# Computing both halves of V for three chunks ahead, and turning the fourth x chunk by a DMA

## The chip, the cores and the metric

One core of a Trainium2 chip. The metric is the device time of one execution in microseconds (us); the span in a profile is the time from its first to its last instruction, some 1.7 us less. Kernels that ran once are of unknown state: their times are told, but what follows is taken from their traces, with the granted clock of TensorE (the share of its full speed that the chip allowed it) where it matters. In lines of a profile, PE is TensorE and PEld its weight loads, ACT is ScalarE, DVE VectorE, POOL GpSimd, and SPq the queue that issues the DMAs; a timeline line gives the start and the duration in us, and in brackets the idle time before it and what ended it.

## The reference, cut to what matters

```python
h  = x + A(layernorm(x))          # memory-augmented attention, 32 heads of 32, 4 segments of 512 tokens
h2 = h + B(layernorm(h))          # gated MLP with a 2048 x 2048 spatial mix
# inside A, for the 2048 tokens of width 1024:
q = x @ wq ; k = x @ wk ; v = x @ wv
# per segment: causal softmax(q k^T) v, mixed with a memory read, memory updated; then o @ wo
```

All tensors are bf16. Segment 0 consists of four chunks of 128 tokens; each has to be normalized and turned (transposed) before Q, K and V of it can be computed.

## The kernel before

The kernel writes down operations in program order with their reads and writes; TensorE keeps that order, the other engines get a fixed order from a list scheduler. The start stage is a string, one word per piece of TensorE work: `T`/`t` is a half chunk turned by four TensorE transposes (copied out by VectorE or ScalarE), `v20` is the first of eight matmuls of chunk 2 with the first half (512 columns) of wv.

```python
LOAD = '12ab3'          # x1, x2, first wv half in two pieces, x3 (x0 goes ahead of them)
START = 'T00 t01 v00 v01 v02 v03 t10 T11 v04 ... v07 v10 ... v14 T20 T21 v15 ... v24 T30 T31 v25 v26 v27 v30 ... v37'
# ...
w_half(WQ, A_wq, 0)
w_half(WK, A_wk, 0)
w_half(WV, A_wv, 1)     # second wv half, last
```

The attention stage is a loop over 16 pairs (a, b) of head groups. Each pair has five steps, and each step begins with logits into PSUM banks 0 to 3, which ScalarE reads in one exponential. Groups of eight matmuls that are not urgent (`v_group`, `wo_group`) fill the steps:

```python
def logits(parts):                      # L464: row-tiled matmuls into banks 0..3
    ...
    act(o, src, ACTF.Exp, scale=float(SCALE))     # one exponential of 128 x 2048

FILL = [  # groups, and the slot (after which step) of each
    (vf((0, 0, 1)) + vf((0, 1, 1)) + vf((0, 2, 1)) + vf((0, 3, 1), eng=DVE), (0, 1, 2, 4,)),   # pair 0
    (vf((1, 0, 0)) + vf((1, 0, 1), eng=DVE), (2, 4,)),                                          # pair 1
    # ...
]
for pair in range(16):
    logits([(a, 0, 0)]);              Pq(b); filler(0);  X(a - 1)             # step 1
    logits([(a, 1, 128), (a, 3, 0)]); Pk(b); MZU(a - 1); phi(b); filler(1)    # step 2
    chores(a)                         # with n < 4: x_norm(4 + n); x_turn(4 + n)
    logits([(a, 2, 0), (b, 2, 256)]); Pq(b + 1); filler(2)                    # step 3
    logits([(b, 0, 0)]);              Pk(b + 1); phi(b + 1); X(a); filler(3)  # step 4
    logits([(b, 1, 128), (b, 3, 0)]); MZU(a); filler(4)                       # step 5
```

(Conditions for the first and last pair are cut. X and MZU are the products with V and the memory update, many matmuls of 33 or 132 columns.)

The softmax here doesn't subtract the row's maximum and nothing guards it: scores larger than these inputs give would overflow.

## Time and profile before

| | before |
|---|---|
| median of the first 3 runs | 796.34 us (796.32 to 800.05) |
| span of the profile | 794.5 us |
| TensorE busy | 99%, granted clock 1.000 |
| TensorE waits in the trace | 2.3 us, all before 9.52 us |
| first logits | 20.03 us |

A table of busy shares says little here, since TensorE is busy all the time.

### The profile page before, as it was taken

Reading aid. Unit: us, or ns where it says so; the run is one execution under the profiler, and the core shown is the slowest. Engines: PE = TensorE matmul, PEld = TensorE weight load, DVE = VectorE, ACT = ScalarE, POOL = GpSimd, SP = SyncE. Lnnn points to the kernel's source line nnn. Section 1 sums busy time; section 2 is a strip of 40 time slices with the busy share of each in tenths; the row PEclk is TensorE's granted clock in tenths of the full one; section 3 lists DMA queues with packets and bytes.
Section 4 is the critical chain, followed back from the end, with each engine's and each line's share of the span. In section 5 each row is a group of like instructions: output and inputs, shape, how many; then the busy total and the mean of one; then the engine's idle time right before and its main releaser. Section 6 shows DMA issues by size and latency. Waiting matters only on the chain.

```text
span 794.5 us, 12077 instructions
## 1 busy us (share of the span) xinstructions
PE 789.9 (99%) x5377; PEld 322.2 (41%) x4773; DVE 373.1 (47%) x857; ACT 289.8 (36%) x341; POOL 140.1 (18%) x266
## 2 busy tenths in 40 slices
PE   8999999999999999999999999999999999999998
PEld 3455554555554542341322314443244334424433
DVE  5784788768765686804215051132233223322322
ACT  5788977777778862132323323100000000000000
POOL 0454535433443341200001010000000000000000
PEclk9999999999999999999999999999999999999999
DMA  9677524622423658510000116603310530011001
GB/s 302 147 142 172 136 54 87 136 65 69 86 54 87 173 124 211 157 40 1 1 0 1 31 34 156 184 1 82 106 32 1 119 100 1 0 55 60 0 1 54
DMA packets 128471, 64.77 MB, mean 82 GB/s; under 512 B 95520, under 2 KB 120352, under 8 KB 128416
## 3 DMA queue, kind: packets, MB, share of 16 engines
q1 hardware_dynamic: 128416, 63.99, 32.7%
q8 instruction: 40, 0.66, 0.3%
q14 instruction: 15, 0.12, 0.1%
HBM read 32.51 MB, written 8.39 MB: 51 GB/s over the span
## 4 chain that ended last, share of the span: by engine, by line
PE 99%; DMA 1%; SPq 0%; issue 0%; DVE 0%
PE ps L327 81%; PE ps L328 14%; PE ps L464 3%; DMA wv<-in_A_wv_dram 1%; SPq L516 0%; PE ps L468 0%; DVE hx L495 0%
## 5 line engine op out<-in xcount | busy, mean ns | idle before, releaser
L327 PE MATMUL ps<-wspT,z 128*128 128x512 bf16 x896 | 194.0, 379 | 0.0
L473 ACT ACTIVATE e<-ps 128x2048 bf16<-128x2048 f32 x80 | 149.8, 1873 | 40.0 <-PE ps L464 40.0
L327 PEld LDWEIGHTS ps<-wspT,z 128*128 128x128 bf16 x896 | 87.7, 98 | 106.4 <-issue 1.0
L473 ACT ACTIVATE z<-ps 128x512 bf16<-128x512 f32 x120 | 63.1, 571 | 145.4 <-PE ps L327 145.4
L495 DVE TENSOR_TENSOR tg<-ps,brow 128x512 bf16<-128x512 f32 x56 | 38.7, 692 | 149.9 <-PE ps L327 122.6
L698 POOL TENSOR_SCALAR_AFFINE_SELECT e<-e 128x1024 bf16<-128x1024 bf16 (+1 forms) x80 | 77.3, 967 | 133.4 <-ACT e L473 133.1
L327 PE MATMUL ps<-hnT,win 128*128 128x512 bf16 x448 | 97.3, 379 | 0.0
L328 PE MATMUL ps<-win,hnT 128*128 128x512 bf16 (+1 forms) x384 | 90.1, 344 | 0.0
L327 PE MATMUL ps<-wout,y 128*128 128x512 bf16 (+2 forms) x252 | 85.8, 367 | 0.0
L568 DVE BATCH_NORM_STATS2 stats<-z 128x6 f32<-128x448 bf16 x64 | 40.1, 627 | 97.0 <-ACT z L473 95.4
L495 DVE TENSOR_TENSOR hx<-hx,ps 128x512 bf16<-128x512 bf16 (+1 forms) x65 | 42.2, 674 | 81.6 <-PE ps L327 81.4
L328 PE MATMUL ps<-wout,y 128*128 128x512 bf16 x210 | 79.6, 379 | 0.0
L327 PEld LDWEIGHTS ps<-hnT,win 128*128 128x128 bf16 x448 | 43.8, 98 | 54.2 <-issue 2.0
L327 PE MATMUL ps<-wv,xnT 128*128 128x512 bf16 x256 | 60.3, 379 | 1.1 <-DMA wv<-in_A_wv_dram 1.1
L327 PE MATMUL ps<-xnT,wk 128*128 128x512 bf16 (+2 forms) x264 | 60.8, 374 | 0.0
L327 PE MATMUL ps<-xnT,wq 128*128 128x512 bf16 x256 | 60.8, 380 | 0.0
L327 PE MATMUL ps<-wo,oT 128*128 128x512 bf16 x256 | 58.8, 379 | 0.0
L327 PEld LDWEIGHTS ps<-wout,y 128*128 128x128 bf16 x252 | 24.2, 98 | 72.2 <-issue 69.1
L327 PE MATMUL ps<-win,hnT 128*128 128x512 bf16 x128 | 48.5, 379 | 0.0
L327 PEld LDWEIGHTS ps<-win,hnT 128*128 128x128 bf16 x128 | 12.5, 98 | 81.4 <-issue 80.9
L327 PEld LDWEIGHTS ps<-v,e 128*128 128x128 bf16 x1280 | 40.1, 96 | 9.8 <-issue 1.7
L327 PE MATMUL ps<-v,e 128*128 128x33 bf16 x1280 | 42.1, 177 | 0.0
(72 smaller groups left out, 609.6 us busy)
## 6 DMA issues: line engine op xcount, KB each, us to landing
win<-in_B_w_in_dram SPq DMA_DIRECT2D x6, 1024.0 KB, 5.3
hx<-in_A_x_dram SPq DMA_DIRECT2D x16, 256.0 KB, 2.8
out_dram<-hx SPq DMA_DIRECT2D x16, 256.0 KB, 2.3
hx<-out_dram SPq DMA_DIRECT2D x16, 256.0 KB, 2.6
out_dram<-hx SPq DMA_DIRECT2D x31, 128.0 KB, 1.7
xin<-in_A_x_dram SPq DMA_DIRECT2D x15, 256.0 KB, 4.0
wout<-in_B_w_out_dram SPq DMA_DIRECT2D x2, 1792.0 KB, 10.1
wq<-in_A_wq_dram SPq DMA_DIRECT2D x2, 1024.0 KB, 7.3
```

What stands on the lines that cost most here:

```text
L327: return e.matmul(out, lhsT, rhs, start=start, stop=stop)
L328: return e.add_instruction(mybir.InstMatmult(name="I-%d" % (1000000 + o.idx), engine=e.engine, ins=[e.lower_ap(rhs), e.lower_ap(lhsT)], ou ...
L464: G.op(PE, lambda e: e.matmul(o, lhsT, rhs, start=True, stop=True, tile_position=(32 * i, 0)), [lhsT, rhs], [o], n / 2.4 if last else 3.5, ...
L473: G.op(ACT, lambda e: e.activation(o, i, func, scale=scale, **kw), r, [o], ((172 if inps(i) else 224) + n_of(i)) / 1.2 + 26, prio=prio, na ...
L495: G.op(DVE, lambda e: e.tensor_tensor(o, a, b, op), [a, b], [o], vcost(o, [a, b], fast), name="tt", prio=late[0])
L568: G.op(DVE, lambda e, si=si, so=so: e.bn_stats(so, si), [si], [so], (cs + 143) / 0.96, name="bn_stats", prio=late[0])
L698: G.op(POOL, lambda e: e.affine_select(d, d, pat, ALU.is_ge, 0.0, base=0, channel_multiplier=-1), [d], [d], 1270 if j else 640, name="mask")
```

## The change

Its intent: let three second-half V groups do in the start what they did among the fillers, and use the time that they take to turn chunk 3 by a DMA instead of on TensorE. For that the second wv half is loaded earlier, the transpose is issued ahead of wk, and chunks 4 to 7 are normalized and turned ahead of pair 0. The filler lists are shifted to fit.

```diff
-    LOAD = '12ab3'
+    LOAD = "12ab3h"                       # h: second wv half
-    START = '... v24 T30 T31 v25 v26 v27 v30 ... v37'
+    START = '... v24 v25 v26 v27 u00 ... u07 u10 ... u17 u20 ... u27 v30 ... v37'
     w_half(WQ, A_wq, 0)
-    w_half(WK, A_wk, 0)
-    w_half(WV, A_wv, 1)
     dma(BETAB[:], A_beta.partition_broadcast(128))
 ...
+    x_turn(3)                             # DMA transpose of chunk 3
+    w_half(WK, A_wk, 0)
+    G.ops[-1].deps.add(first[3] + 5)      # wk waits for chunk 3's norm, so it queues behind the transpose
 ...
     for tc in range(4, 8):
         x_load(tc)
+        G.ops[-1].deps.add(first[3] + 5)
+    for tc in range(4, 8):
+        x_norm(tc)
+        x_turn(tc)
     FILL = [
-        (vf((0, 0, 1)) + vf((0, 1, 1)) + vf((0, 2, 1)) + vf((0, 3, 1), eng=DVE), (0, 1, 2, 4,)),
-        (vf((1, 0, 0)) + vf((1, 0, 1), eng=DVE), (2, 4,)),
+        (vf((0, 3, 1)) + vf((1, 0, 1), eng=DVE) + vf((1, 0, 0)), (0, 1, 4,)),
 ...                                       # 52 groups before, 49 after
```

## The prediction

> **What bounds the kernel now.** I read the page first (busy shares, then the chain that ended last), then what TensorE waited for, then the timeline of the first 45 us, then the DMA issues, their landings and the bytes moved in 2 us stretches.
>
> ```profile
> span 794.5 us, 12077 instructions
> PE 789.9 (99%) x5377; PEld 322.2 (41%) x4773; DVE 373.1 (47%) x857; ACT 289.8 (36%) x341; POOL 140.1 (18%) x266
> ...
> PE 99%; DMA 1%; SPq 0%; issue 0%; DVE 0%
> ```
>
> The chain that ended last is TensorE for 99% of the span. Busy is modelled, so I checked it with TensorE's own waits over the whole run, of which there are only two kinds:
>
> ```profile
> PE ps L327 <- DVE zero L531: 1.2, 1, 1.2
> PE ps L327 <- DMA wv<-in_A_wv_dram: 1.1, 2, 0.7
> ```
>
> Both lie before 9.52 us. From there on the start stage, which the change rewrites, is gapless (view: timeline of TensorE):
>
> ```profile
> 9.52 2.12 PE L327 MATMUL ps<-wv,xnT 128*128 128x512 bf16 x9 [0.35 <-DMA wv<-in_A_wv_dram]
> 11.47 0.61 PE L468 MATMUL ps<-ident,xin 128*128 128x128 bf16 x8
> 11.91 1.89 PE L327 MATMUL ps<-wv,xnT 128*128 128x512 bf16 x8
> 13.64 0.61 PE L468 MATMUL ps<-ident,xin 128*128 128x128 bf16 x8
> 14.09 2.54 PE L327 MATMUL ps<-wv,xnT 128*128 128x512 bf16 x11
> 16.46 1.89 PE L327 MATMUL ps<-xnT,wq 128*128 128x512 bf16 x8
> ```
>
> Read the starts, not the durations, which overlap: 8 matmuls of 512 columns take 13.64 - 11.91 = 1.73 us, 216 ns each; the 8 transposes of chunk 3 take 14.09 - 13.64 = 0.45 us, 56 ns each. The attention stage is as tight. I cut it into steps at the logits (line L464). With 16 wide matmuls a step always takes 3.88 to 3.90 us; with 8 of them and 24 of 33 columns 2.75 or 2.76; a filler group of 8 always adds 1.73. Steps of equal content never differ by more than 0.02 us up to 288 us, so nothing waits there. Here are two kinds of step, and ScalarE in them (timeline, some rows left out):
>
> ```profile
> 27.81 0.40 PE L464 MATMUL ps<-qk 32*128 32x256 bf16 x8
> ...
> 28.14 1.90 PE L327 MATMUL ps<-xnT,wq 128*128 128x512 bf16 x8
> ...
> 29.87 1.89 PE L327 MATMUL ps<-wv,xnT 128*128 128x512 bf16 x8
> ...
> 31.70 0.39 PE L464 MATMUL ps<-qk 32*128 32x512 bf16 x4
> ...
> 37.25 0.39 PE L464 MATMUL ps<-qk 32*128 32x512 bf16 x4
> ...
> 37.70 1.88 ACT L473 ACTIVATE e<-ps 128x2048 bf16<-128x2048 f32 x1 [0.40 <-PE ps L464]
> ```
>
> The step from 27.81 to 31.70 holds one Q group and one filler. The last two lines give the second bound of a step: the exponential starts 0.45 us after its logits and takes 1.88, and the next logits go into the same four PSUM banks.
>
> **What the Trainium skill says.** "TensorE: Matmul & The Clock Gate", section "Wait — 56ns, not 53.3ns?": warm matmuls start every columns / 2.4 GHz plus about 2.5 ns, 55.6 ns at 128 columns and 215.7 at 512. The trace agrees (56 and 216 ns). The same page, "Part 4: PE-mode transpose", gives about 275 ns for a transpose in a kernel. The page of this profile has a mean of 243 ns for them, but in a train only 56 ns pass from one to the next, so 0.45 us is what eight of them cost. "DMA: Bandwidth & Descriptors", section "Queues, rings and completion order": each DMA engine consumes its ring's descriptors in order. The trace agrees: adding up bytes in issue order predicts the landings (below). "Perfetto Trace Analysis", section "DMA Instruction — HWDGE (DVE, Sync)": a DMA's recorded span is the issue only, not the movement; here the wk load is 1.71 us long in the queue's timeline and lands 11.5 us after its issue.
>
> **The change part by part.** (1) Removed from TensorE: T30 and T31, 8 transposes: -0.45 us. Two DVE copies of 0.42 us go too, off the path. (2) Moved: three V groups, u0, u1 and u2 (24 matmuls, 24 x 216 ns = 5.18 us), from the filler lists to the start. I counted the lists: 52 filler groups before, 49 after. So the start grows by 5.18 us, the attention pairs shrink by 5.18 us, net zero as long as every step stays bound by TensorE. (3) Added: one DMA transpose of x chunk 3, off TensorE if it lands in time. (4) The loads are reordered: second wv half, wq, then the transpose, then wk and x chunks 4 to 7.
>
> Does (3) or (4) make TensorE wait? Queue and bytes before:
>
> ```profile
> 2.64 0.98 SPq L516 DMA_DIRECT2D wv<-in_A_wv_dram  x2
> 3.67 0.51 SPq L516 DMA_DIRECT2D xin<-in_A_x_dram  x1
> 4.21 0.43 SPq L516 DMA_DIRECT2D wq<-in_A_wq_dram  x1
> 4.69 1.71 SPq L516 DMA_DIRECT2D wk<-in_A_wk_dram  x1
> 6.44 3.90 SPq L516 DMA_DIRECT2D wv<-in_A_wv_dram  x1
> ```
>
> The 2 us stretches move 15, 241, 324, 299, 349, 376, 349, 348, 348 and 375 GB/s from 0 to 20 us. Summed, 3.15 MB (x0 to x3, first wv half, wq) has gone by 11.8 us and wq landed at 4.21 + 9.0 = 13.2; 4.19 MB by 14.8, and wk landed at 4.69 + 11.5 = 16.2; 5.24 MB by 17.9, and the second wv half landed at 6.44 + 12.7 = 19.1. So a landing is the byte count plus 1.3 us. New order, as estimates from these numbers:
> - second wv half takes wq's place: lands 13.2. u00 is due when v27 ends: 13.64 + 3 x 0.216 = 14.29. Margin 1.1 us.
> - wq takes wk's place: 16.2, due at 21.2. Harmless.
> - the transpose can issue when chunk 3 is normalized, at 12.76 + 0.55 = 13.31 (now followed by the x loads at 13.36). wq's bytes are ahead of it until 14.8, 1.4 us. Transposes of such a chunk land 3.1 at least and 3.4 us in the median after their issue, so it lands at 16.5 to 18.2. v30 is due at 14.29 + 5.18 = 19.47. Margin 1.3 us or more.
> - wk: 1.05 MB at 0.35 MB/us behind the transpose: about 20.3; due at 19.47 + 2 x 1.73 = 22.93. Margin 2.6 us.
> - x chunk 4 about 21, normalized in some 3.3 us (statistics 1.4, aggregate 0.2, GpSimd 0.8, scale 0.55, hand-overs), transposed by about 28; its first reader, the filler of pair 0's second step, is due at about 30.8. VectorE has almost nothing from 15 to 20 us (0.32 us of 5).
>
> Every margin is positive. The first logits move from 20.03 to 20.03 - 0.45 + 5.18 = 24.76.
>
> (5) The one new wait. Pair 0 had fillers in steps one, two, three and five; now in one, two and five. Its third step keeps only the Q group: 3.89 - 1.73 = 2.16 us on TensorE, a length that no step has before (minimum 2.75). The exponential needs 0.45 + 1.88 = 2.33 us, plus a hand-over which I put at 0.05 to 0.2 us. So TensorE waits 0.2 to 0.4 us there; I take 0.3. All other pairs keep a filler in their third and fifth step, and their shortest steps are 2.75 us with one exponential, as in the pairs of 15.0 us that show no wait now.
>
> Sum: -0.45 (transposes) + 0.3 (pair 0, third step) = -0.15 us. From 796.34 that is 796.2.
>
> **The rivals.** A: the transpose is late. Against it the margin of 1.3 us; for it that landings up to 8.0 us are seen when several transposes and a load share the engines, as at 30 to 42 us. A landing 8 us after issue, 21.3, would cost 1.9 us: about 798. B: the early normalization of chunks 4 to 7, now ahead of pair 0 in the program, puts VectorE's in-order queue in front of the Q copies and stalls the first pairs. For it: VectorE's statistics of chunk 4 start right after the landing at 20 us now, so it does wait for data there. Against it: VectorE is idle just then, and first logits come 4.7 us later. If it happens, 0.5 to 2 us: 797 to 798. C: ScalarE becomes the bound in the thinner pairs (three fillers instead of four in pairs of segments 1 and 2). An estimate for such a pair: 5 exponentials 9.4, four copies of 0.6, two phi exponentials of about 1.05, up to three V copies of 0.6 make 15.7 us, against 17.2 of TensorE. It should hold, with less slack than before; losses of 0.1 us in several pairs would make 797. D: the intent as one may read it, that starting V early fills holes of the start. The waits view speaks against it: the 1.1 us on wv lie before the first V group that the change moves, and its loads are not touched. No more than the 0.45 us is to be had: 795.9.
>
> **Range and chances.** All terms are under 2 us, 2% is 15.9 us. The middle is 796.2; the low end 795.4 is D and a little run to run difference (two of three runs of before agree within 0.02 us, one was 3.7 above); the high end 797.8 leaves room for A, B or C. Faster by over 2%: 1%. Slower by over 2%: 1%. Within: 98%.
>
> **What would show it.** Right: the 8 transposes at 13.64 gone, one train of 8 + 3 + 24 + 8 = 43 wide V matmuls from 11.91 without a gap, first logits at 24.7 to 24.8, third step of pair 0 at 2.4 to 2.5 us with TensorE's weight load waiting on the exponential, then the same step lengths as before and PE waits unchanged. Wrong: a wait on xnT or wv inside the V train (A, or the 1.1 us margin), a wait on a VectorE copy in pairs 0 and 1 (B), steps of equal content that differ by over 0.05 us later (C), or first logits before 24.5 us (D and more).

## The result, and the profile after

| | runs | median us | range |
|---|---|---|---|
| before | 6 | 796.63 | 796.05 to 800.05 |
| changed | 6 | 796.16 | 795.86 to 797.75 |

The ratio of changed to before is 0.999, with a 95% interval of 0.9973 to 1.0008. A ratio is the mean time of one kernel's fast runs over that of the other's from the same rounds, so it isn't quite the ratio of the medians. The two can't be told apart by their times. The predicted 796.2 lies 0.04 us from the median; with runs that spread over 2 to 4 us that closeness is luck, and the steps have to be judged in the traces.

The page of the changed kernel, span, busy shares and the chain that ended last:

```profile
span 794.4 us, 11964 instructions
PE 783.0 (99%) x5273; PEld 321.3 (40%) x4765; DVE 369.4 (47%) x854; ACT 290.6 (37%) x342; POOL 138.7 (17%) x266
...
PE 96%; DVE 2%; issue 1%; ACT 1%; DMA 0%; POOL 0%; SPq 0%
```

TensorE shows 104 instructions fewer, but only 8 were taken out. The rest are records that the trace lost: in most steps one wide matmul is missing (seven listed where the program has eight), and the step is as long as ever. A missing record leaves 0.2 us "idle", which the view of waits puts down to whatever ended nearby:

```profile
PE ps L327 <- DVE ra L502: 1.9, 12, 0.2
...
PE ps L327 <- DMA wv<-in_A_wv_dram: 0.5, 1, 0.5
...
PE ps L464 <- ACT e L473: 0.2, 1, 0.2
```

The twelve waits of 0.2 us on `ra` are such holes, and so, it seems, is the lower share of TensorE in the chain: the trace of experiment 3, the same program but for the slot of one filler, has all 5,369 records, no wait on `ra`, and TensorE at 98% of its chain. The last line is real. The timeline of TensorE in the start:

```profile
11.51 0.61 PE L468 MATMUL ps<-ident,xin 128*128 128x128 bf16 x8
11.95 9.44 PE L327 MATMUL ps<-wv,xnT 128*128 128x512 bf16 x42
21.23 1.89 PE L327 MATMUL ps<-xnT,wq 128*128 128x512 bf16 x8
22.96 1.91 PE L327 MATMUL ps<-xnT,wk 128*128 128x128 bf16 x16
24.80 0.40 PE L464 MATMUL ps<-qk 32*128 32x512 bf16 x4
```

The transposes at 13.64 are gone. One train of 43 wide matmuls (42 recorded) runs from 11.95 to 21.23: 9.28 us, 216 ns each, so no wait on wv or on chunk 3. First logits at 24.80 against 24.76 predicted. And pair 0's third step, with ScalarE (other rows left out):

```profile
32.58 0.40 PE L464 MATMUL ps<-qk 32*128 32x256 bf16 x8
32.91 1.90 PE L327 MATMUL ps<-xnT,wq 128*128 128x512 bf16 x7
33.03 1.88 ACT L473 ACTIVATE e<-ps 128x2048 bf16<-128x2048 f32 x1 [0.65 <-PE ps L464]
34.95 0.10 PEld L464 LDWEIGHTS ps<-qk 32*128 32x128 bf16 x4 [0.64 <-ACT e L473]
34.96 0.40 PE L464 MATMUL ps<-qk 32*128 32x512 bf16 x4 [0.15 <-ACT e L473]
```

The logits begin at 32.58, the exponential 0.45 later at 33.03, it ends at 34.91, and the next logits begin 0.05 us after that. The step took 2.38 us where TensorE had work for 2.16. All other steps have the length that a step of the same content had before (2.75, 2.80, 3.03, 3.89, 4.48, 4.76) within 0.02 us.

To compare traces whose starts differ, I count from S, the start of the transposes of chunk 2, which both kernels have and which lies behind the last wait on wv:

| from S to | before | changed | difference |
|---|---|---|---|
| (S itself) | 11.47 | 11.51 | |
| first logits | 8.56 | 13.29 | +4.73 |
| pair 0, fourth step | 20.23 | 23.45 | +3.22 |
| first matmul of the MLP stage | 281.89 | 281.66 | -0.23 |

4.73 is 5.18 - 0.45. In pair 0 the lost filler gives 1.73 back, less 0.22. By the MLP stage all moved groups cancel, and what stays is -0.45 + 0.22 = -0.23 us. It stays to the end: the device time of the profiled execution less S is 796.26 - 11.47 = 784.79 us before and 796.08 - 11.51 = 784.57 changed, 0.22 less.

### The profile page after: what moved, and what is told of

Same layout as the page of the kernel before. It is cut to its first block, busy times and chain, and to the rows that moved or that the text cites. A ratio compares the mean times of both kernels' runs of the same rounds, so it can differ in the third digit from the quotient of the medians.

```text
span 794.4 us, 11964 instructions
## 1 busy us (share of the span) xinstructions
PE 783.0 (99%) x5273; PEld 321.3 (40%) x4765; DVE 369.4 (47%) x854; ACT 290.6 (37%) x342; POOL 138.7 (17%) x266
## 4 chain that ended last, share of the span: by engine, by line
PE 96%; DVE 2%; issue 1%; ACT 1%; DMA 0%; POOL 0%; SPq 0%
PE ps L327 78%; PE ps L328 15%; PE ps L464 3%; ACT e L473 0%; DMA xin<-in_A_x_dram 0%; DVE stats L570 0%; DVE xin L489 0%; DVE hx L495 0%; DVE pkt L498 0%; ACT hx L587 0%; PE ps L468 0%; DVE oq L495 0%; SPq L516 0%; DVE v L485 0%; ACT hx L585 0%
## 5 line engine op out<-in xcount | busy, mean ns | idle before, releaser
L327 PE MATMUL ps<-wout,y 128*128 128x512 bf16 (+2 forms) x243 | 82.5, 367 | 0.0
L327 PE MATMUL ps<-xnT,wk 128*128 128x512 bf16 (+2 forms) x249 | 57.4, 373 | 2.4 <-DVE ra L502 1.9
L327 PE MATMUL ps<-wv,xnT 128*128 128x512 bf16 x239 | 57.2, 380 | 1.4 <-DMA wv<-in_A_wv_dram 0.5
L327 PE MATMUL ps<-wo,oT 128*128 128x512 bf16 x244 | 57.1, 379 | 0.6
L327 PE MATMUL ps<-win,hnT 128*128 128x512 bf16 x122 | 46.3, 380 | 0.0
L509 POOL TENSOR_SCALAR rs<-mv 128x1 f32<-128x1 f32 x44 | 10.8, 246 | 192.9 <-DVE mv L573 192.9
```

The source lines that it names most:

```text
L327: return e.matmul(out, lhsT, rhs, start=start, stop=stop)
L509: G.op(POOL, lambda e: e.tensor_single_scalar(o, i, s, op), [i], [o], 220 if n_of(o) < 8 else 220 + 2.5 * n_of(o), name="pts1", prio=late[0])
```

## The experiments

One run of the kernel before, timed beside numbers 1 to 4, took 797.74 us, and one beside numbers 5, 6, 8 and 11 took 796.06.

**1. The V group of chunk 3 ahead of the moved groups.** What do the moved groups cover, and when does the transpose land?

```diff
-START = '... v27 u00 ... u27 v30 ... v37'
+START = '... v27 v30 ... v37 u00 ... u27'
```

> The changed kernel with one edit: the V group of chunk 3 stands before the three moved groups u0 to u2, so nothing hides the DMA transpose. Theory (the moved groups are there to cover the transpose; it lands 16.5 to 18.2 us after the start): TensorE is due at chunk 3 at about 14.33 us and waits for xnT for 2.2 to 3.9 us, and the first logits move from 24.80 to 27.0 to 28.7 us. Rival (the transpose is in by then, its place does not matter): no wait, first logits at 24.8.

Measured: 799.89 us in one run, with first logits at 28.61. Timeline of TensorE:

```profile
10.93 0.61 PE L468 MATMUL ps<-ident,xin 128*128 128x128 bf16 x8
11.38 2.54 PE L327 MATMUL ps<-wv,xnT 128*128 128x512 bf16 x11
16.44 8.77 PE L327 MATMUL ps<-wv,xnT 128*128 128x512 bf16 x32 [2.52 <-DMA xnT<-xin]
25.04 1.89 PE L327 MATMUL ps<-xnT,wq 128*128 128x512 bf16 x8
```

TensorE was due at 11.38 + 11 x 0.216 = 13.76 and began at 16.44: a gap of 2.68 us. The queue issued the transpose at 12.79, so it landed within 3.65 us of its issue, in the range of the prediction. In the changed kernel the issue is at 13.37 and the landing, which the trace also records, 3.7 us later at 17.1; v3 is due at 11.95 + 35 x 0.216 = 19.51: 2.4 us to spare. The moved groups are what hides the transpose. The first logits lie within the 27.0 to 28.7 expected, but not for the reason given: S came 0.6 us early, and the stretch from S grew by 4.39 us, not by the 2.68 of the wait. The 32 matmuls from 16.44 to 25.04 took 8.60 us where 6.91 is usual. The windows by two us show why (after the length come the busy times of PE, PEld, DVE, ACT and POOL, then granted clock, DMA share and GB/s):

```profile
14.00:16.00 2.00, 0.00 (x0) 0.00 (x0) 0.00 (x0) 1.03 (x4) 0.00 (x0) 1.00 1.26 282
16.00:18.00 2.00, 1.56 (x5) 0.63 (x6) 1.60 (x8) 0.02 (x1) 0.00 (x0) 0.72 0.94 291
18.00:20.00 2.00, 2.00 (x6) 0.73 (x5) 0.42 (x3) 0.34 (x1) 0.00 (x0) 0.50 1.08 386
20.00:22.00 2.00, 2.00 (x10) 0.80 (x8) 1.11 (x2) 0.47 (x2) 0.00 (x0) 0.92 0.88 327
```

TensorE's clock fell to half after the wait. In windows of 1 us it is 0.94, three times 0.50, and 0.85 from 16 to 21 us, which makes 0.12 + 3 + 0.30 = 3.4 us at half clock and 1.7 us lost, the 4.39 - 2.68. That the wait was the reason was a new theory, so it got its own run (number 5).

**2. Chunk 3 turned on TensorE again, the rest as changed.**

```diff
-START = '... v24 v25 v26 v27 u00 ...'
+START = '... v24 T30 T31 v25 v26 v27 u00 ...'
-    x_turn(3)
```

> The changed kernel with chunk 3 turned by TensorE again (8 transposes, 2 copies), all else as changed. Theory (the only saving in the start is the spacing of 8 transposes, 8 x 56 ns): the first logits come at 24.80 + 0.45 = 25.25 us, the third step of pair 0 stays at 2.38 us, and the attention stage is otherwise shifted by 0.45 us. Rival 1 (a transpose costs its own duration of 243 ns): 24.80 + 1.9 = 26.7. Rival 2 (the saving is in the new order of loads and groups): 24.8.

Measured: 798.77 us in one run, and first logits at 27.50, past all three numbers. The absolute times don't serve, because this run started late: it waited 2.60 us for the first wv half, and its clock, too, fell to 0.50 from 9 to 12 us. Counted from S:

```profile
13.76 0.61 PE L468 MATMUL ps<-ident,xin 128*128 128x128 bf16 x8
14.20 1.89 PE L327 MATMUL ps<-wv,xnT 128*128 128x512 bf16 x8
15.93 0.61 PE L468 MATMUL ps<-ident,xin 128*128 128x128 bf16 x8
16.38 7.72 PE L327 MATMUL ps<-wv,xnT 128*128 128x512 bf16 x35
...
27.50 0.40 PE L464 MATMUL ps<-qk 32*128 32x512 bf16 x4
```

First logits come 27.50 - 13.76 = 13.74 us after S, against 13.29 in the changed kernel, so +0.45. Third step of pair 0: 35.28 to 37.66, 2.38 us. From S to the MLP stage 282.10, +0.44. So the eight transposes cost their spacing of 56 ns each, and the start holds no other gain.

**3. The filler of the second step moved to the third.** This tells the exponential from the K and Q copies as the cause of the 0.22 us.

```diff
-        (vf((0, 3, 1)) + vf((1, 0, 1), eng=DVE) + vf((1, 0, 0)), (0, 1, 4,)),
+        (vf((0, 3, 1)) + vf((1, 0, 1), eng=DVE) + vf((1, 0, 0)), (0, 2, 4,)),
```

> The changed kernel with the filler of pair 0's second step moved to its third step. Theory (a step cannot be shorter than logits to exponential, the exponential, and the hand-over to the next logits): the third step is 3.89 us again, and the second step, now 2.16 us of TensorE work, takes 2.5 us, since there the V copy of the step before holds the exponential back to 0.60 us after its logits (0.60 + 1.87 + 0.06). Rival (the wait of 0.22 us in the third step belongs to what that step reads, the Q and K copies of the second head group): the second step is 2.16 us, and the sum of the two is 0.2 us less than now.

Measured: 796.66 us in one run. Timeline of TensorE and ScalarE:

```profile
28.96 0.40 PE L464 MATMUL ps<-qk 32*128 32x384 bf16 x8
29.07 0.60 ACT L473 ACTIVATE v<-ps 128x512 bf16<-128x512 f32 x1 [0.97 <-PE ps L327]
...
29.56 1.87 ACT L473 ACTIVATE e<-ps 128x2048 bf16<-128x2048 f32 x1
31.32 0.67 ACT L473 ACTIVATE qk<-ps 128x256 bf16<-128x256 f32 x2
31.48 0.10 PEld L464 LDWEIGHTS ps<-qk 32*128 32x128 bf16 x4 [0.79 <-ACT e L473]
31.49 0.56 PE L464 MATMUL ps<-qk 32*128 32x256 bf16 x8 [0.30 <-ACT e L473]
```

The second step took 31.49 - 28.96 = 2.53 us: the exponential starts 0.60 after the logits, behind the V copy, runs 1.87, and 0.06 passes. That is the theory. But the rival had a part that I had denied it: the third step took 4.05 us instead of 3.89, since its second four logits need the K copy of the step before, which can now start only when the exponential is through. So a starved second step costs 0.37 + 0.16 us, against 0.22 for a starved third one. Of these two steps the change had left the cheaper one bare.

**4. The old order of loads.**

```diff
-LOAD = "12ab3h"
+LOAD = "12ab3"
 w_half(WQ, A_wq, 0)
+w_half(WK, A_wk, 0)
+w_half(WV, A_wv, 1)
 ...
 x_turn(3)
-w_half(WK, A_wk, 0)      # with its wait on chunk 3's norm
```

> The changed kernel with the loads in the old order (wq, wk, then the second wv half, the transpose of chunk 3 behind them). Theory (loads land in issue order at the byte count plus 1.3 us): the second wv half lands at 19.1 us, u00 is due at 14.33 and waits 4.8 us, the transpose behind it lands before v3 is due at about 24.3, and the first logits come at 29.6 us. Rival (the loads share the engines and land together, or the order is of no weight): a wait under 1 us, first logits at 24.8 to 25.8.

Measured: 803.63 us in one run. TensorE was due at u00 at 12.49 + 11 x 0.216 = 14.87 and began at 19.65, 4.78 us later. The wait is the one predicted from the byte count (4.8), though both of its ends came half a us later than expected (the half landed at 19.6, not 19.1). The first logits came at 32.35, not at 29.6, or 20.30 from S: 7.01 more than in the changed kernel. Of that 4.78 is the wait and 2.2 the clock, which the theory had left out and which the windows show at 0.50 from 18 to 24 us. Without the new order of loads the rest of the change would lose 7 us.

**5. Number 1 with the array kept busy over the wait.**

```diff
-START = '... v27 v30 ...'
+START = '... v27 W v30 ...'      # W: 11 matmuls of a zero tile into a bank that nobody reads
```

> The run with v3 ahead of u0 to u2 again, with 11 idle matmuls on a zero tile (2.4 us) put into the wait for the transpose. Times from the start of the transposes of chunk 2 to the first logits: 13.29 us in the changed kernel, 17.68 with v3 first, of which 2.68 is the gap before v3 and 1.7 a slower V train behind it, at a granted clock of 0.5. Theory (the clock was halved because TensorE had stood idle for over 2.5 us, and the wait itself costs only its length): with the array kept busy the clock stays at 1.00 and the stretch takes 13.29 + 2.7 = 16.0 us. Rival (the slow train comes from the transfers beside it, or from the V groups' operands): it stays at 17.7 us.

Measured: 798.83 us in one run; from S (11.38) to the first logits 27.54 - 11.38 = 16.16 us, against 17.68 in number 1. The same windows:

```profile
14.00:16.00 2.00, 2.00 (x11) 0.09 (x1) 0.00 (x0) 1.26 (x3) 0.00 (x0) 1.00 1.20 255
16.00:18.00 2.00, 1.69 (x9) 0.48 (x6) 1.20 (x6) 0.23 (x1) 0.00 (x0) 1.00 0.98 294
18.00:20.00 2.00, 2.00 (x11) 0.90 (x10) 0.83 (x6) 0.60 (x1) 0.00 (x0) 1.00 1.06 373
```

The clock stays at 1.00, and the 32 matmuls behind the wait take 23.97 - 17.05 = 6.92 us. Useless matmuls in a wait saved 1.5 us. The Trainium skill, "TensorE: Matmul & The Clock Gate", section "What's actually happening", says that the array goes back to half clock after an idle window of about 3.4 us, and needs a busy one as long to return, the windows running freely. The runs agree in the return: half clock lasted 3.4 us in numbers 1, 2, 6, 7 and 11, and twice that in number 4. For the fall, the length of a wait alone doesn't decide: it followed waits of 1.76 (number 6), 2.60 (2), 2.68 (1) and 2.84 us (11), but not waits of 1.79 (the trace of number 9) and 2.89 us (the first of number 7). Windows that run freely would do that, depending on where a wait lies in them; no run here tests it.

**6. The transpose behind the wk load.**

```diff
-    x_turn(3)
     w_half(WK, A_wk, 0)
-    G.ops[-1].deps.add(first[3] + 5)
+    x_turn(3)
```

> The changed kernel with the wk load issued ahead of the transpose of chunk 3. Theory (in issue order, 1.05 MB at 0.35 MB per us ahead of it add 3 us): the transpose lands at about 19.4 us instead of 16.4, v3 is due about 19.5, so TensorE waits 0 to 0.5 us; from the start of chunk 2's transposes to the first logits 13.3 to 13.8 us. Rival (the transpose has far more room, or passes other transfers): 13.29, and no wait on xnT. If the wait is above 1 us the margin was smaller than I think.

Measured: 797.96 us in one run; no wait on xnT, 13.30 us from S to the first logits. The missing wait decides nothing: this run waited 1.8 us for the first wv half, with the clock down, and reached S only at 13.39, so v3 was due at 13.84 + 35 x 0.216 = 21.4, two us behind the expected landing. The landings in the trace decide more. wk, issued at 10.81, landed 8.9 us later at 19.7, and the transpose, issued at 15.25, 5.3 later at 20.5 (17.1 in the changed kernel). It did not pass the load. In a start as usual v3 is due at 19.5; an estimate, with the 0.5 us by which this run's loads were late (wq landed at 16.6, not 16.1) taken off, is a landing at 20.0 and a wait of half a us. Number 7 repeats it with more in front.

**7. The transpose behind both halves of wk.**

```diff
-    x_turn(3)
     w_half(WK, A_wk, 0)
-    G.ops[-1].deps.add(first[3] + 5)
+    w_half(WK, A_wk, 1)
+    x_turn(3)
```

> The changed kernel with both halves of wk (2.1 MB) issued ahead of the transpose of chunk 3; the run with one half could not decide, as its start was 1.9 us late and v3 due as much later. Theory (issue order, 0.35 MB per us): the transpose lands about 6 us later than 16.4, at 22.4; v3 is due at 19.5 in a start as usual, so TensorE waits 2 to 3 us, less where the start is late, and above 2.5 us the clock falls to 0.5 as with v3 first and costs up to 1.7 more. Rival (the transpose passes the loads): no wait.

Measured: 802.59 us in one run. The start was late again (S at 12.76), v3 due at 13.21 + 35 x 0.216 = 20.77, begun at 24.32: 3.55 us of wait, more than I had said, and the V and Q groups behind it 1.7 us slow at the half clock. (The 2.89 us wait for wv early in the same run left the clock at 1.00, so the 2.5 us of the expectation is no threshold.) The queue:

```profile
11.69 3.30 SPq L516 DMA_DIRECT2D wk<-in_A_wk_dram  x2
15.03 5.56 SPq L516 DMA_TRANSPOSE xnT<-xin  x1
```

The issue of the transpose took 5.56 us instead of 1.3, with the loads in front still moving. That is not where the extra wait came from: the second half of wk landed at 23.4 and the transpose at 24.3, 0.9 us behind it, as far as in number 6, where the issue took 1.49. What was late is all the loads of this run (wq landed at 17.5, where the changed kernel has 16.1), which with the expected 22.4 makes 23.8. The transpose does not pass the loads. With two such loads in front the change's order of transpose and wk is needed; with one, by number 6, it is likely worth some half a us, which is not shown.

**8. u2 back among the fillers of pair 0.** This undoes the one loss that the change has.

```diff
-START = '... u17 u20 ... u27 v30 ...'
+START = '... u17 v30 ...'
-        (vf((0, 3, 1)) + vf((1, 0, 1), eng=DVE) + vf((1, 0, 0)), (0, 1, 4,)),
+        (vf((0, 2, 1)) + vf((0, 3, 1)) + vf((1, 0, 1), eng=DVE) + vf((1, 0, 0)), (0, 1, 2, 4,)),
```

> The changed kernel with u2 back among pair 0's fillers, which now has one in steps one, two, three and five. Theory (the third step's extra 0.22 us is the exponential's, and a filler hides it): from the start of chunk 2's transposes to the first logits 13.29 - 1.73 = 11.56 us, steps one to three 3.89 each, and to the fourth step of pair 0 11.56 + 11.67 = 23.23 us instead of 23.45, so 0.22 less; the transpose, landing 3.6 us after its issue, is in 0.8 us before v3 is due at about 17.8. Rival 1 (the transpose is late with one group less in front of it): a wait on xnT of up to 1 us in front of v3, and 23.4 to 24.2 in all. Rival 2 (another wait takes the place): no gain, 23.45.

Measured: from S (11.54) first logits 11.57 us, steps of 3.89, 3.89 and 3.88, fourth step 23.23, all as expected, no wait on the transpose; to the MLP stage 281.44 us. 795.89 us in one run.

**9 and 10. The changed kernel and version 8, timed with five rounds** on one chip (no edit).

> The changed kernel as it is, timed again. By the steps its work is 0.19 us shorter than before's once the start has begun alike (0.45 saved, 0.22 spent in pair 0's third step, 0.04 in the start), while single runs of either kernel spread over 2 us and more. Theory (the spread comes from when the first wv half lands, which the change does not touch): ratio 0.999 to 1.001, not told from 1; from the start of chunk 2's transposes to the fourth step of pair 0 23.45 us. Rival (the change also moves the start): a ratio outside that.

> The version with four fillers in pair 0, timed. By the steps 0.22 us shorter than the changed kernel and 0.41 shorter than before, 0.05% of the span: median 0.2 to 0.6 us under before, ratio 0.999 to 1.000, most likely not told from 1 by the interval. From the start of chunk 2's transposes to the fourth step of pair 0 23.23 us.

| | runs | median us | range | ratio to before | 95% interval | S | S to MLP stage |
|---|---|---|---|---|---|---|---|
| before | 11 | 796.59 | 795.72 to 798.62 | | | 11.47 | 281.89 |
| changed (9) | 6 | 796.55 | 795.79 to 798.14 | 0.9998 | 0.9984 to 1.0012 | 11.76 | 281.66 |
| four fillers (10) | 6 | 796.08 | 795.46 to 796.78 | 0.9992 | 0.9979 to 1.0006 | 11.09 | 281.44 |

(S and what follows for before are of its first profile; each other row is of its own profile.) The stretch from S repeats to 0.01 us between the two traces of the changed kernel and between the two of version 8. By that count version 8 is 0.45 us faster than before and 0.22 faster than the change. The whole executions say the same once S is taken off their device time: 784.79 us before, 784.57 and 784.59 changed, 784.35 and 784.37 with four fillers. So what spreads in these is S, not the rest. By the clock on the wall version 8 has the lowest median, and the interval still holds 1: not shown faster.

**11 and 12. A second chunk turned by DMA.** If eight transposes are worth 0.45 us, eight more may be.

```diff
-LOAD = "12ab3h"
+LOAD = "12ab3i"                                   # i: rows 0..3 of 8 of the second wv half
-START = '... v10 ... v14 T20 T21 v15 v16 v17 v20 ... v27 u00 ... u27 v30 ...'
+START = '... v10 ... v17 u00 ... u03 u10 ... u13 v20 ... v27 u04 ... u07 u14 ... u17 u20 ... u27 v30 ...'
-    w_half(WQ, A_wq, 0)
-    x_turn(3)
+    x_turn(2)
+    wv_rows(4, 8, 512)                            # rest of the second wv half, then wq,
+    w_half(WQ, A_wq, 0)                           # both waiting for chunk 2's norm
+    x_turn(3)
```

> The changed kernel with chunk 2 turned by a DMA too, behind the first four rows of the second wv half, the rest of that half and wq behind it; u0 and u1 begin before v2. Theory (8 transposes fewer on TensorE save their spacing, if every landing is hidden): from the start of chunk 1's transposes to the first logits 15.90 us now, 15.45 then; chunk 2 lands about 13 us and is due at 13.9. Rival 1 (the queue is held up: a landing is late by a fraction of a us up to 2 us): 15.6 to 17.4, with a wait on xnT or wv. Rival 2 (wk or x chunk 4 now land late for pair 0): first logits at 15.45 but a wait on wk or xnT in the first steps.

The first try gave 800.65 us in one run: a 2.8 us wait for the first wv half with half clock after it, and 1.60 us on the transpose of chunk 4 in pair 0's second step. The queue had issued chunk 3's transpose only at 18.26, because ScalarE had beta's exponential ahead of chunk 3's square root. (It was not waiting for beta, as the next expectation says: that landed at 13.4. From 14.32 to 17.14 it loaded a table in 1.28 us, did the exponential in 0.23 and loaded a table in 1.28 again; the input of the square root was there at 14.0, and it began at 17.16.) The second try loads beta behind wq, which moves the exponential too:

> Two chunks turned by DMA, with the beta load moved behind wq, because the trace of the first try shows ScalarE waiting for beta ahead of the square root of chunk 3's norm, so that chunk 3's transpose was issued at 18.26 us and all behind it late. Theory (with that mended the turns are hidden and 8 more transposes save their spacing): from the start of v04 to the fourth step of pair 0 25.41 us in the changed kernel, 24.96 here, no wait on xnT; time 0.45 us under the changed kernel. Rival (the queue has no room for a second transpose: the gap until chunk 2 is normalized puts everything behind it back): 25.5 to 27, with a wait on xnT or wv.

Measured: median 798.41 us of 6 runs (798.16 to 800.68), ratio 1.0025 with an interval of 1.001 to 1.0039: slower than before, under the 2% of a verdict. From v04 (9.33) to the fourth step of pair 0 (37.06): 27.73 us, past the rival's 25.5 to 27. The waits of TensorE and the queue:

```profile
PE ps L327 <- DMA xnT<-xin: 2.4, 2, 1.6
```

```profile
12.71 3.11 SPq L516 DMA_TRANSPOSE xnT<-xin  x1
15.86 0.59 SPq L516 DMA_DIRECT2D wk<-in_A_wk_dram  x1
16.50 3.63 SPq L516 DMA_DIRECT2D xin<-in_A_x_dram  x4
27.47 1.20 SPq L516 DMA_TRANSPOSE pk<-pkt  x1
28.71 3.03 SPq L516 DMA_TRANSPOSE xnT<-xin  x2
```

Chunk 3's transpose is held 3.11 us in its issue behind wq and beta and lands at 19.8, 1.0 us behind wq, and TensorE waits 0.84 for it. Chunk 4's is issued at 28.71, in the fixed order of the queue behind a transpose of the first pair, where the changed kernel has it at 24.66; TensorE waits 1.59. That the queue has no room for a second transpose in any order is not shown.

## Why the prediction was right, point by point

- **The bound.** Right: each step of attention but pair 0's third has the length that its content had before, within 0.02 us.
- **(1) -0.45 us for the transposes.** Shown by number 2: +0.45 when they come back. The rival reading, 243 ns each, would have been 1.9 us.
- **(2) The moved groups cancel.** Right to the rounding: +5.18 in the start, -0.23 left at the MLP stage.
- **(3) and (4) All landings in time.** Right, landing by landing. The trace of the changed kernel has the second wv half at 13.2 us (13.2 said), wq at 16.1 (16.2), the transpose at 17.1 (16.5 to 18.2), wk at 20.5 (20.3), x chunk 4 at 21.2 (21) and its transpose at 27.7 (28). In number 4 the byte count gave the wait for the second wv half (4.8 expected, 4.78 measured), and numbers 6 and 7 show the order of the queue. A full queue also holds the issue itself, which the sum leaves out; the landings of numbers 6 and 7 show no cost of it.
- **(5) +0.3 us in pair 0's third step.** Right in kind, and in the stated 0.2 to 0.4: 0.22 measured. I had put the hand-over at 0.05 to 0.2; it is 0.05. Numbers 3 and 8 show that the exponential is the cause; number 3 also shows a second one, the K copy behind it, where the step before is the starved one.
- **The sum.** -0.15 said, -0.23 measured from S to the MLP stage.
- **The rivals.** A, B and C did not happen: no wait on xnT (2.4 us to spare, where 1.3 or more was said), first reader of chunk 4 on time, no stretched step. (A's cost of 1.9 us is 21.3 - 19.47 = 1.8 by its own numbers.) D's reading (holes of the start filled) is refuted by number 2.
- **The range.** It held, but its reason for the spread was thin ("a little run to run difference"). The spread has a cause that the traces show: S, as in numbers 9 and 10 and in the list below.

## What to carry to other kernels

Where one engine is busy throughout, compare start times of equal steps: they show 0.05 us that no timing of whole runs will. A piece moved within the bound engine's queue was worth nothing by itself here; it is worth the removed work minus the waits of the steps that it leaves too short, so look for the shortest step that any engine can keep up with (here 0.45 + 1.88 + 0.05 = 2.38 us) before taking a filler away. And count landings in issue order, bytes over rate, before putting a transfer where TensorE will meet it.

## What the Trainium skill lacked or had wrong

- "TensorE: Matmul & The Clock Gate", "Back-to-back issue gap": a stream of weight loads and matmuls is put at about 81 ns for 128 columns and 131 for 512. In these runs, with a weight load per matmul, it is 56 and 216 ns (8 transposes in 0.45 us, 43 V matmuls in 9.28 us), which is what the same page's section "Wait — 56ns, not 53.3ns?" gives.
- The same page, "Part 4: PE-mode transpose": about 275 ns in a kernel is no price for one of a train. Eight more cost 0.45 us, 56 ns each (number 2).
- The same page, "What's actually happening": an idle window of about 3.4 us is named for the fall to half clock, but not how idle it has to be. Waits of 1.76 to 2.84 us were followed by the fall in four runs, waits of 1.79 and 2.89 us were not (number 5 lists them). The fall cost 1.7 us on top of the wait in number 1, 2.2 in number 4. Waits in the start, with the fall or without, make the run to run noise: S lay between 10.93 and 13.76 us in twelve traces whose kernels all begin with the same loads, and the three latest (12.76, 13.39, 13.76) had waits of 2.9, 1.8 and 2.6 us on the first wv half.
- "DMA: Bandwidth & Descriptors": the sections read here give no number for how far an issue is held by a full queue. Issue of a transpose of one chunk took 1.3 us when the transfers in front were to land within 2.9 us (changed kernel), 1.49 at 4.4 us (number 6), 3.11 at 6.3 (number 12) and 5.56 at 8.4 (number 7).
- The pages on reading a profile don't have this: trace records of matmuls can be missing (96 of 5,369 in the changed kernel's profile), and the holes are shown as waits of 0.2 us on unrelated instructions.
